# GpSimd's scale placed behind its low half, and norm weights as scalar operands, in a kernel for linear attention and a mixture of experts

## Chip, cores and metric

One core of one Trainium2 chip. The metric is the device time of one execution in microseconds (us). TensorE is PE in the profile, VectorE DVE, ScalarE ACT, GpSimd POOL, SyncE SP.

## The reference

Two parts in a row. Attention without softmax, for batch 8, 8 heads, 576 positions, head size 64:

```python
kv = np.einsum('bhsd,bhse->bhde', k, v)
out = np.einsum('bhsd,bhde->bhse', q, kv)
rms = np.sqrt(np.mean(out * out, axis=-1, keepdims=True) + 1e-06)
attn = out / rms * g_norm            # g_norm: 64 weights
```

The heads are put beside each other, which gives 4608 rows `x` of 512. Then a mixture of 8 experts: each row goes to the expert with the largest `x @ w_gate`, an expert takes at most 1152 rows, and a row's output is

```python
gate_w * (np.maximum(x @ w1[e], 0) @ w2[e])      # w1: 512 x 1024, w2: 1024 x 512
```

## The kernel before, in words

**First stage (to about 160 us).** For each batch PE makes `kv`, then the attention rows and the expert logits; VectorE and GpSimd work out the norm and the routing; each finished row goes to a scratch tensor `x_dram` in HBM as 8 heads of 64 un-normed values, each with its norm factor beside it. Rows of the expert that is picked first are worked on early.

**Second stage.** The experts are ranked by their number of rows and given fixed budgets of 704, 672, 640, 624, 592, 576, 560 and 512 rows (line 19). Experts are counted by `r` from 0. While the products of expert `r` run, two things are prepared for expert `r + 1`:

- `rows_beside` (line 1591), for tiles of 128 rows. Five steps for each tile: GpSimd gathers it with an indirect DMA into `xg` (`fetch`, line 437, four buffers); GpSimd scales it by the norm factors into `xm` (`norm`, line 444, a two-tensor product, two buffers; for `r` = 1 VectorE may do it) and copies the gate column (`gate`, line 453); ScalarE casts `xm` to float16, the high half of `pair` (`pair_high`, line 471, two buffers); GpSimd subtracts that from `xm`, the low half (`pair_low`, line 476); SyncE issues a transposing DMA from `pair` into `xs` (`pair_turn`, line 481).
- `weights` (line 1540), for `w1` and `w2`: eight pieces of 128x512 float32 each. VectorE takes the maximum of each piece (`top`, line 344, `am`); `most` (line 350) reduces the eight to one per partition, `a`, and for `w1` multiplies it by `gcol`, the column of norm weights; PE turns `a` into a row (`across`, line 357), VectorE reduces that to one number `bm` (line 361), PE spreads it to all partitions (`back`, line 364), and VectorE makes a power of two from it (`scale`, line 366), for `w1` multiplied by `gcol` again (`sg`, line 373). Then ScalarE casts each scaled piece to float16 (`high`, line 378, `w1h`, `w2h`) and VectorE makes the rest (`low`, line 384, `w1l`, `w2l`).

The products (line 1626): for each of eight blocks `j` of the hidden size PE sums three terms into a bank `hp` (line 532; two banks), ScalarE takes the relu in float16 (`hh`, line 537), and VectorE the rest (`hl`, line 540, which reads `hp` from PSUM and `hh` from SBUF). Then PE makes the tiles of the second product `yp` (lines 578 and 587), ScalarE scales them (line 603), GpSimd scatters the rows to the output (line 608).

**What sets the order.** No engine's order is chosen at run time. Each stage lists its operations with an engine, a planned duration, dependencies, a key and buffers held in rings; `Plan.place` (line 112) goes through them in planned time and always starts what can start first on an engine, by the smaller key and then by the earlier entry where several can. What it finds is the fixed order of all five instruction streams, the DMA issues on SP and POOL among them. An added dependency so changes the planned time of what follows, and with it the order of any engine from there on. The hardware still waits on semaphores where data demand it. The planned durations of the two steps on GpSimd are 1.22 us (`NORM`) and 1.33 us (`PAIR`).

Of the kernel before, what the change touches and what calls it, by code (L numbers as in the profile page):

```python
# [15 lines left out]
ALU = mybir.AluOpType  # L16
# [65 lines left out]
class Ring:  # L82
# [3 lines left out]
    def new(self):  # L86
        self.holds.append(Hold(self.holds[-self.n] if len(self.holds) >= self.n else None))
        return self.holds[-1]
# [8 lines left out]
class Plan:  # L97
# [5 lines left out]
    def op(self, ways, fn, deps=(), key=0.0, takes=(), uses=(), late=0.0):  # L103

        ways = [ways] if isinstance(ways[0], str) else list(ways)
        o = Op(ways, fn, [d for d in deps if d is not None], list(takes), key, late)
        for h in takes + uses if isinstance(takes, tuple) and isinstance(uses, tuple) else list(takes) + list(uses):
            h.users.append(o)
        self.ops.append(o)
        return o  # L110
# [56 lines left out]
def attention_moe_kernel(  # L167
# [12 lines left out]
    nc = tc.nc  # L180
# [79 lines left out]
    gcol = cst.tile([P, 1], F32, name="gcol")  # L260
# [25 lines left out]
    first = cst.tile([P, E], F32, name="first")  # L286
# [12 lines left out]
    def exponent(src, least, name, pool=sm):  # L299

        e = pool.tile([P, 1], I32, name=name)
        nc.vector.tensor_scalar(out=e, in0=src.bitcast(I32), scalar1=23, scalar2=None, op0=ALU.logical_shift_right)
        nc.vector.tensor_scalar(out=e, in0=e, scalar1=least, scalar2=None, op0=ALU.max)
        return e

    def pow2(e, mul, add, name, pool=sm):

        t = sm.tile([P, 1], I32, name="p2t")
        nc.vector.tensor_scalar(out=t, in0=e, scalar1=mul, scalar2=add, op0=ALU.mult, op1=ALU.add)
        r = pool.tile([P, 1], I32, name=name)  # L310
        nc.vector.tensor_scalar(out=r, in0=t, scalar1=23, scalar2=None, op0=ALU.logical_shift_left)
        return r.bitcast(F32)
# [18 lines left out]
    def split_weight(i, ws, raw, pieces=8):  # L331

        z = {}
        m = KD * F // pieces
        wh, wl = ws[2 * i], ws[2 * i + 1]
        sl = lambda p: slice(p * m, (p + 1) * m)

        def am():
            if "am" not in z:
                z["am"] = sm.tile([P, pieces], F32, name=f"am{i}")  # L340
            return z["am"]

        def top(p):
            nc.vector.tensor_reduce(out=am()[:, p:p + 1], in_=raw[:, sl(p)], axis=AX.X, op=ALU.max,  # L344
                                    apply_absolute_value=True)

        def sum(p):
            nc.scalar.activation(wl[:, sl(p)], raw[:, sl(p)], AF.Abs, accum_out=am()[:, p:p + 1])

        def most():  # L350
            z["a"] = a1 = sm.tile([P, 1], F32, name=f"a1_{i}")
            nc.vector.tensor_reduce(out=a1, in_=am(), axis=AX.X, op=ALU.max)
            if i == 0:
                nc.vector.tensor_tensor(out=a1, in0=a1, in1=gcol, op=ALU.mult)

        def across(pt):
            nc.tensor.transpose(pt[0:1, 0:P], z["a"], ident)  # L357

        def across_max(pt):
            z["m"] = sm.tile([1, 1], BF16, name="bm")  # L360
            nc.vector.tensor_reduce(out=z["m"], in_=pt[0:1, 0:P], axis=AX.X, op=ALU.max, apply_absolute_value=True)

        def back(pb):
            nc.tensor.matmul(pb[:, 0:1], lhsT=ones_bf, rhs=z["m"], start=True, stop=True)  # L364

        def scale(pb):
            z["b"] = sm.tile([P, 1], F32, name="bmax")
            nc.vector.tensor_copy(z["b"], pb[:, 0:1])
            z["e"] = exponent(z["b"], 30, f"ew{i}")
            z["s"] = pow2(z["e"], -1, (256, 268)[i], f"sw{i}")  # L370
            if i == 0:
                sg = sm.tile([P, 1], F32, name="sg")
                nc.vector.tensor_tensor(out=sg, in0=z["s"], in1=gcol, op=ALU.mult)  # L373
                z["s"] = sg

        def high(p, e="A"):
            if e == "A":
                nc.scalar.activation(wh[:, sl(p)], raw[:, sl(p)], AF.Copy, scale=z["s"])  # L378
            else:
                nc.gpsimd.tensor_scalar(out=wh[:, sl(p)], in0=raw[:, sl(p)], scalar1=z["s"], scalar2=None, op0=ALU.mult)  # L380

        def low(p, e="V"):
            if e == "V":
                nc.vector.scalar_tensor_tensor(out=wl[:, sl(p)], in0=raw[:, sl(p)], scalar=z["s"], in1=wh[:, sl(p)],  # L384
                                               op0=ALU.mult, op1=ALU.subtract)
            else:
                nc.gpsimd.tensor_scalar(out=raw[:, sl(p)], in0=raw[:, sl(p)], scalar1=z["s"], scalar2=None, op0=ALU.mult)
                nc.gpsimd.tensor_tensor(out=wl[:, sl(p)], in0=raw[:, sl(p)], in1=wh[:, sl(p)], op=ALU.subtract)

        return dict(top=top, sum=sum, most=most, across=across, across_max=across_max, back=back, scale=scale, high=high, low=low), z  # L390

    def split_steps(i, ws, raw, psum_pool, tag, pieces=8):
# [24 lines left out]
    def spans(s0, s1):  # L417

        cuts = [s0] + list(range((s0 // P + 1) * P, s1, P)) + [s1]
        return [(a, b - a, NHI if a % P else a // P) for a, b in zip(cuts, cuts[1:])]  # L420
# [215 lines left out]
    def slots(pool, reg_ap, s0=0):  # L636

        c_reg = nc.vector.value_load(reg_ap, min_val=0, max_val=(E - 1) * NHI)
        both = []
        for tab_, nm in ((gidx_tab, "gi"), (sidx_tab, "si")):  # L640
            t = pool.tile([P, NHI + 1], I32, name=f"{nm}{s0}", bufs=3)
            nc.vector.tensor_copy(t[:, 0:NHI], tab_[:, ds(c_reg, NHI)])  # L642
            if s0 % P:
                nc.vector.tensor_copy(t[0:P - s0 % P, NHI:NHI + 1], t[s0 % P:P, s0 // P:s0 // P + 1])
            both.append(t)
        return both
# [23 lines left out]
    op = plan.op  # L670
# [860 lines left out]
    op = plan.op  # L1531
# [59 lines left out]
    def rows_beside(r, key):  # L1591

        hold, sl, st = new("xs"), new("slots"), {}

        def cut(e):
            st["gi"], st["si"] = slots(mo, perm_i[0:1, 1, r:r + 1])

        cut_ = op(("V", 0.4), cut, [early["rank"]], key, (sl,))
        n = len(spans(0, BUDGET[r]))
        gates, turned, first, sent, asked = [], [], None, [], []  # L1600
        for i in range(n):
            xg, xm, pair = new("xg"), new("xm"), new("pair")

            def fetch(e, i=i):
                if i == 0:
                    st["x"] = Rows(mo, st["gi"], 0, BUDGET[r], BM, 4)
                st["x"].fetch(i)

            o = op(("P", 1.05), fetch, [cut_, first] + early.get(("lows", r - 1), [])[-1:], key, (hold, xg), (sl,))
            first = first or o  # L1610
            asked.append(o)
            o = op(("D", GATHER), None, [o], key, (), (xg,))
            a = op([("V", 0.61), ("P", NORM)] if r == 1 else ("P", NORM),
                   lambda e, i=i: st["x"].norm(i, nc.vector if e == "V" else nc.gpsimd), [o], key - 5 if r == 1 else key + 1,
                   (xm,), (xg,))
            gates.append(op(("P", 0.25), lambda e, i=i: st["x"].gate(i, nc.gpsimd), [a], key + 1, (), (xg, hold)))
            a = op(("A", 0.52), lambda e, i=i: st["x"].pair_high(i), [a], key + 1, (pair,), (xm, hold))
            a = op(("P", PAIR), lambda e, i=i: st["x"].pair_low(i), [a], key + 1, (), (xm, pair, hold))
            if r == 1:
                early.setdefault(("lows", r), []).append(a)  # L1620
            a = op(("S", TURN), lambda e, i=i: st["x"].pair_turn(i), [a], key + 1, (), (pair, hold))
            sent.append(a)
            turned.append(op(("D", TURNED), None, [a], key + 1, (), (pair, hold)))
        return st, hold, sl, gates, turned, sent, asked
# [50 lines left out]
    o = op(("S", 0.01), moved, [early["scaled"]], -9 * KEY, (), tuple(ews))  # L1675
# [6 lines left out]
    for r in range(E):  # L1682
        products(r, *args)
        key = KEY * r
        if r + 1 < E:
            before = [] if r > 1 else sent
            st, xs_hold, sl, gates, turned, sent, asked = rows_beside(r + 1, key + ROWS)
# [3 lines left out]
        else:  # L1691
            steps, o = plan_rest(), early["later"]
            for _ in range(68):
                o = op(("V", 0.2), lambda e: next(steps, None), [o], key + 1)
# [36 lines left out]
```

## Time and profile before

| | us |
|---|---|
| median of 3 runs | 568.02 (567.17 to 572.36) |
| profiled execution, its own time | 568.83 |
| span of its profile | 567.0 |
| PE busy | 520.8 (92%) |
| VectorE busy | 383.5 (68%) |
| ScalarE busy | 251.3 (44%) |
| GpSimd busy | 218.6 (39%) |

The span runs from the first to the last instruction. Busy time of PE is modelled and its records overlap a little, so a high share says that it is fed, not that it is at its peak. In a timeline the columns are the start, the time from there to the end of the last of the merged instructions, engine, line of the source, operation, tiles, shapes and count; in brackets stand the idle time of the engine just before and what ended it. [...]

### The profile page before, as it was taken

How to read it: one execution, taken by the hardware profiler on the slowest of the kernel's cores; microseconds unless marked ns; L12 is line 12 of the kernel's file. 1: busy time of each engine (PE TensorE's matmuls, PEld its weight loads, DVE VectorE, ACT ScalarE, POOL GpSimd, SP SyncE). 2: the span in 40 equal slices, each digit the busy share in tenths (PEclk: the TensorE clock that was granted, in tenths of full speed). 3: DMA queues.
4: the chain of work that ended last, by engine and by line, in shares of the span. 5: the costliest groups of instructions: out<-in, count | busy, mean ns of one | idle time of the engine just before them, and what ended most of it. 6: DMA issues, size and time to landing. Idle time of an engine off the chain costs nothing.

```text
span 567.0 us, 12425 instructions
## 1 busy us (share of the span) xinstructions
PE 520.8 (92%) x4727; PEld 342.4 (60%) x4727; DVE 383.5 (68%) x1009; ACT 251.3 (44%) x496; POOL 218.6 (39%) x288
## 2 busy tenths in 40 slices
PE   4999796887988997998999999999999999999994
PEld 4888685764536564544664576487467648745442
DVE  4487788999949989999998195456729606721200
ACT  1757583876313651653724435252534425202210
POOL 3012525543155583746234730644373171012011
PEclk9989996999999997999999999999999999999998
DMA  8999999654168687696947472774556151011010
GB/s 272 376 349 319 357 396 373 214 191 187 79 196 278 161 274 201 148 342 116 284 131 218 104 233 58 193 181 150 160 145 209 44 112 41 2 38 39 0 39 30
DMA packets 78020, 102.60 MB, mean 181 GB/s; under 512 B 43222, under 2 KB 51414, under 8 KB 76932
## 3 DMA queue, kind: packets, MB, share of 16 engines
q1 hardware_dynamic: 69600, 70.43, 42.8%
q0 software_dynamic: 7776, 31.30, 15.7%
q8 instruction: 39, 0.64, 0.5%
q14 instruction: 25, 0.20, 0.1%
q10 hardware_dynamic: 580, 0.02, 0.1%
HBM read 73.13 MB, written 20.61 MB: 165 GB/s over the span
## 4 chain that ended last, share of the span: by engine, by line
PE 25%; issue 15%; DMA 5%; DVE 3%; POOL 1%; ACT 1%; POOLq 0%; DVEq 0%; ACTq 0%
PE yp L578 12%; PE hp L532 12%; DMA out_dram<-ysb,si 5%; PE yp L587 1%; DVE w2l L384 1%; POOL xg L440 1%; DVE hl L540 1%; ACT w1h L378 0%; ACT w2h L378 0%; POOL xm L448 0%; POOLq L1666 0%; POOL pair L478 0%; POOL out_dram L608 0%; PE pt_max L357 0%; PE pt_max L364 0%
## 5 line engine op out<-in xcount | busy, mean ns | idle before, releaser
L532 PE MATMUL hp<-xs,w1h 128*128 128x320 f16 (+6 forms) x896 | 135.2, 303 | 4.2 <-DVE hl L540 4.2
L532 PEld LDWEIGHTS <-w1h 128*128 128x128 f16 x960 | 93.8, 99 | 48.5 <-issue 8.6
L608 POOL DMA_INDIRECT out_dram<-ysb,si x41 | 42.7, 1042 | 135.7 <-ACT ysb L603 100.0
L578 PEld LDWEIGHTS <-hh 128*128 128x128 f16 x560 | 54.4, 98 | 65.5 <-issue 3.1
L537 ACT ACTIVATE hh<-hp 128x320 f16<-128x320 f32 (+7 forms) x64 | 40.8, 638 | 113.2 <-PE hp L532 113.1
L344 DVE TENSOR_REDUCE am<-raw 128x1 f32<-128x512 f32 x120 | 75.7, 674 | 3.4 <-DMA raw<-in_moe_w_dram 3.4
L532 PE MATMUL hp<-xs,w1l 128*128 128x320 f16 (+6 forms) x448 | 72.1, 301 | 0.0
L478 POOL TENSOR_TENSOR pair<-xm,pair 128x512 f16<-128x512 f32 (+5 forms) x35 | 44.1, 1262 | 67.6 <-ACT pair L474 62.9
L540 DVE SCALAR_TENSOR_TENSOR hl<-hp,hh 128x320 f16<-128x320 f32 (+7 forms) x64 | 47.2, 737 | 32.8 <-ACT hh L537 32.6
L578 PE MATMUL yp<-w2h,hh 128*128 128x512 f16 x272 | 64.4, 379 | 0.8 <-ACT ysb L603 0.8
L578 PE MATMUL yp<-w2l,hh 128*128 128x512 f16 x272 | 64.6, 379 | 0.0
L603 ACT ACTIVATE ysb<-yp,ysc 128x512 f32<-128x512 f32 (+5 forms) x40 | 27.4, 685 | 83.8 <-PE yp L578 80.0
L578 PE MATMUL yp<-w2h,hl 128*128 128x512 f16 x272 | 64.3, 379 | 0.0
L384 DVE SCALAR_TENSOR_TENSOR w2l<-raw,sw,w2h 128x512 f16<-128x512 f32 x64 | 52.8, 869 | 11.2 <-ACT w2h L378 11.2
L440 POOL DMA_INDIRECT xg<-x_dram,gi x41 | 42.1, 1027 | 44.2 <-DVE gi L642 25.2
L532 PEld LDWEIGHTS <-w1l 128*128 128x128 f16 x480 | 47.0, 98 | 19.5
L825 PE MATMUL op<-kv_bd,qt 128*128 128x144 f32 x256 | 41.9, 303 | 6.4 <-ACT o_sb L678 1.6
L384 DVE SCALAR_TENSOR_TENSOR w1l<-raw,sg,w1h 128x512 f16<-128x512 f32 x64 | 46.7, 783 | 0.9 <-ACT w1h L378 0.8
L578 PEld LDWEIGHTS <-hl 128*128 128x128 f16 x280 | 27.0, 98 | 31.9
L378 ACT ACTIVATE w1h<-raw,sg 128x512 f16<-128x512 f32 x61 | 39.1, 711 | 7.2 <-DVE sg L373 7.1
L378 ACT ACTIVATE w2h<-raw,sw 128x512 f16<-128x512 f32 x62 | 39.6, 710 | 5.0 <-PE yp L587 3.2
L825 PEld LDWEIGHTS op<-kv_bd,qt 128*128 128x128 f32 x256 | 35.3, 198 | 10.0 <-ACT qt L678 2.7
(257 smaller groups left out, 704.2 us busy)
## 6 DMA issues: line engine op xcount, KB each, us to landing
raw<-in_moe_w_dram SPq DMA_DIRECT2D x64, 512.0 KB, 5.0
k_sb<-in_k_dram SPq DMA_DIRECT2D x16, 576.0 KB, 7.3
v_sb<-in_v_dram SPq DMA_DIRECT2D x16, 576.0 KB, 7.2
x_dram<-o_sb POOLq DMA_DIRECT2D x8, 1152.0 KB, 7.4
q_sb<-in_q_dram SPq DMA_DIRECT2D x16, 512.0 KB, 8.1
x_dram<-o_sb POOLq DMA_DIRECT2D x8, 144.0 KB, 7.3
q_sb<-in_q_dram SPq DMA_DIRECT2D x32, 32.0 KB, 6.0
xg<-x_dram,gi POOLq DMA_INDIRECT x41, 4.8
```

The lines of the kernel that those rows point to most:

```text
L344: nc.vector.tensor_reduce(out=am()[:, p:p + 1], in_=raw[:, sl(p)], axis=AX.X, op=ALU.max, apply_absolute_value=True)
L378: nc.scalar.activation(wh[:, sl(p)], raw[:, sl(p)], AF.Copy, scale=z["s"])
L384: nc.vector.scalar_tensor_tensor(out=wl[:, sl(p)], in0=raw[:, sl(p)], scalar=z["s"], in1=wh[:, sl(p)], op0=ALU.mult, op1=ALU.subtract)
L440: nc.gpsimd.indirect_dma_start(out=self.xg[i][0:n], out_offset=None, in_=x_dram[0:self.rows, :], in_offset=bass.IndirectOffsetOnAxis(ap=se ...
L478: nc.gpsimd.tensor_tensor(out=pair[0:n, 1], in0=self.xm[i][0:n], in1=pair[0:n, 0], op=ALU.subtract)
L532: nc.tensor.matmul(self.view(hp)[:, u], lhsT=w[:, c, j * P:(j + 1) * P], rhs=x[:, c, u * hw:(u + 1) * hw], start=(t == 0 and c == 0), stop ...
L537: nc.scalar.activation(self.out(self.hh, j), self.view(hp), AF.Relu)
L540: nc.vector.scalar_tensor_tensor(out=self.out(self.hl, j), in0=self.view(hp), scalar=0.0, in1=self.out(self.hh, j), op0=ALU.max, op1=ALU.s ...
L578: nc.tensor.matmul(yp[0:n, 0:DM], lhsT=h[:, j, o:o + n], rhs=w[:, j, :], start=(m == 0), stop=(m == len(self.terms) - 1))
L603: nc.scalar.activation(self.ysb[0:n], yp[0:n, 0:DM], AF.Copy, scale=self.ysc[0:n, i:i + 1])
L608: nc.gpsimd.indirect_dma_start(out=out[:, :], out_offset=bass.IndirectOffsetOnAxis(ap=self.sidx[0:n, col:col + 1], axis=0), in_=ysb[0:n], ...
L825: nc.tensor.matmul(y, lhsT=qt.t[:, i * P:(i + 1) * P], rhs=kv2[:, half * HH + i], start=True, stop=True)
```

## The change

Two edits. In `split_weight`, the two products of a one-element column with `gcol` are written as `tensor_scalar` with `gcol` as a scalar operand, where they were `tensor_tensor` with `gcol` as a second tensor. In `rows_beside`, for `r` of 2 and above, the scale of tile `i` gets a planned dependency on the low half of tile `i - 1`. Both run on GpSimd for these experts, so it is an order and needs no semaphore of its own. For `r` = 1 nothing is added.

```diff
@@ -351,7 +351,7 @@ most
             if i == 0:
-                nc.vector.tensor_tensor(out=a1, in0=a1, in1=gcol, op=ALU.mult)
+                nc.vector.tensor_scalar(out=a1, in0=a1, scalar1=gcol, scalar2=None, op0=ALU.mult)
@@ -370,7 +370,7 @@ scale
                 sg = sm.tile([P, 1], F32, name="sg")
-                nc.vector.tensor_tensor(out=sg, in0=z["s"], in1=gcol, op=ALU.mult)
+                nc.vector.tensor_scalar(out=sg, in0=z["s"], scalar1=gcol, scalar2=None, op0=ALU.mult)
@@ -1597,7 +1597,7 @@ rows_beside
-        gates, turned, first, sent, asked = [], [], None, [], []
+        gates, turned, first, sent, asked, low = [], [], None, [], [], None
@@ -1611,13 +1611,15 @@
             a = op([("V", 0.61), ("P", NORM)] if r == 1 else ("P", NORM),
-                   lambda e, i=i: st["x"].norm(i, nc.vector if e == "V" else nc.gpsimd), [o], key - 5 if r == 1 else key + 1,
+                   lambda e, i=i: st["x"].norm(i, nc.vector if e == "V" else nc.gpsimd), [o, low], key - 5 if r == 1 else key + 1,
                    (xm,), (xg,))
             gates.append(op(("P", 0.25), lambda e, i=i: st["x"].gate(i, nc.gpsimd), [a], key + 1, (), (xg, hold)))
             a = op(("A", 0.52), lambda e, i=i: st["x"].pair_high(i), [a], key + 1, (pair,), (xm, hold))
             a = op(("P", PAIR), lambda e, i=i: st["x"].pair_low(i), [a], key + 1, (), (xm, pair, hold))
             if r == 1:
                 early.setdefault(("lows", r), []).append(a)
+            else:
+                low = a
```

## Rows read from the trace of the kernel before

**Rows 1.** The page: busy tenths of PE in 40 slices of the span.
```profile
PE   4999796887988997998999999999999999999994
```

**Rows 2.** Waits of PE, 200 to 270 us, then 270 to 562 us.
```profile
PE hp L532 <- DVE hl L540: 3.8, 1, 3.8
PE pt_max L364 <- DVE bm L361: 2.2, 2, 1.2
...
PE pt_max L357 <- DVE a L354: 0.5, 1, 0.5
...
PE hp L532 <- DVE hl L540: 0.3, 1, 0.3
```

**Rows 3.** Windows: length, busy time of PE, PEld, DVE, ACT, POOL; clock, DMA.
```profile
168.80:171.60 2.80, 0.01 (x1) 0.02 (x1) 1.42 (x6) 0.00 (x0) 0.87 (x1) 1.00 1.00 392
...
219.50:225.60 6.10, 6.05 (x24) 3.36 (x24) 6.07 (x12) 0.00 (x0) 0.00 (x0) 0.54 0.52 123
```

**Rows 4.** Timeline of PE, 215 to 269 us: where it waited.
```profile
219.54 4.64 PE L532 MATMUL hp<-xs,w1h 128*128 128x336 f16 x16 [3.82 <-DVE hl L540]
...
258.02 0.27 PE L357 MATMUL pt_max<-ident,a 128*1 128x128 f32 x1 [0.55 <-DVE a L354]
...
261.19 0.16 PE L364 MATMUL pt_max<-bm,ones_bf 1*128 1x1 bf16 x1 [1.17 <-DVE bm L361]
...
268.47 0.16 PE L364 MATMUL pt_max<-bm,ones_bf 1*128 1x1 bf16 x1 [1.06 <-DVE bm L361]
```

**Rows 5.** Timeline of VectorE, 211 to 264 us.
```profile
211.17 6.30 DVE L384 SCALAR_TENSOR_TENSOR w2l<-raw,sw,w2h 128x512 f16<-128x512 f32 x1
...
218.65 0.84 DVE L540 SCALAR_TENSOR_TENSOR hl<-hp,hh 128x672 f16<-128x672 f32 x1
...
232.75 0.64 DVE L373 TENSOR_TENSOR sg<-sw,gcol 128x1 f32<-128x1 f32 x1
...
255.24 2.73 DVE L354 TENSOR_TENSOR a<-a,gcol 128x1 f32<-128x1 f32 x1
257.89 3.04 DVE L344 TENSOR_REDUCE am<-raw 128x1 f32<-128x512 f32 x5
...
263.37 2.65 DVE L373 TENSOR_TENSOR sg<-sw,gcol 128x1 f32<-128x1 f32 x1
```

**Rows 6.** Groups of VectorE by line: shortest, median, longest ns; or busy us, mean ns.
```profile
L354 DVE TENSOR_TENSOR a<-a,gcol x8: 158/160/2730, 91.8 to 412.8; 128x1 f32<-128x1 f32 x8
L373 DVE TENSOR_TENSOR sg<-sw,gcol x8: 159/160/2655, 95.4 to 431.8; 128x1 f32<-128x1 f32 x8
L412 DVE TENSOR_SCALAR ys<-y,y x9: 212/214/215, 145.9 to 522.3; 128x1 f32<-128x1 f32 x9
L569 DVE TENSOR_SCALAR ysc<-gt,ys 128x5 f32<-128x5 f32 x1 | 1.1, 1118 | 0.0
L540 DVE SCALAR_TENSOR_TENSOR hl<-hp,hh x64: 471/760/857, 176.1 to 539.7; 128x320 f16<-128x320 f32 x8, 128x672 f16<-128x672 f32 x8, 128x640 f16<-128x640 f32 x8, 128x624 f16<-128x624 f32 x8
```

**Rows 7.** Timeline of GpSimd, 211 to 266 us.
```profile
211.38 1.07 POOL L448 TENSOR_TENSOR xm<-xg 128x512 f32<-128x512 f32 x1
...
213.55 0.18 POOL L455 COPY gt<-xg 128x1 f32<-128x1 f32 x1
...
214.83 2.09 POOL L448 TENSOR_TENSOR xm<-xg 128x512 f32<-128x512 f32 x2
...
232.23 1.15 POOL L478 TENSOR_TENSOR pair<-xm,pair 128x512 f16<-128x512 f32 x1 [0.44 <-ACT pair L474]
...
255.85 2.10 POOL L448 TENSOR_TENSOR xm<-xg 128x512 f32<-128x512 f32 x2
...
264.94 1.05 POOL L448 TENSOR_TENSOR xm<-xg 112x512 f32<-112x512 f32 x1
```

**Rows 8.** Timeline of ScalarE, 209 to 213 us: the casts of two tiles.
```profile
209.05 0.62 ACT L474 CAST pair<-xm 128x512 f16<-128x512 f32 x1 [0.38 <-POOL xm L448]
...
212.48 0.62 ACT L474 CAST pair<-xm 128x512 f16<-128x512 f32 x1 [2.18 <-POOL xm L448]
```

## The prediction, made before the change was run

> **What bounds the kernel now.** I read the slices of the page first: TensorE (PE) is at nine tenths or more in nearly every slice of the second half, so the question is where it isn't [rows 1]. Its waits by stretch give the answer: from 270 us to the end it waits 0.3 us in all; between 200 and 270 us, where the second expert's products run, it waits on VectorE: 3.8 us for `hl`, 2.2 us for `bm`, 0.5 us for `a` [rows 2]. [...] In PE's order of time the waits are 3.82, 0.55, 1.17 and 1.06 us [rows 4], and 0.3 us follows at 279 us [rows 2]. In all PE loses 3.82 + 2.8 + 0.55 + 1.17 + 1.06 + 0.3 = 9.7 us in a stage that the change touches. From 280 us on nothing can be won, and a delay there has to get through a PE that waits for nobody.
>
> Then I asked why VectorE is late. One `w2l` took 6.30 us from 211.17 us, `a<-a,gcol` on a single element per partition took 2.73 us, `sg<-sw,gcol` 2.65 us [rows 5]; their medians are 0.16 us for the last two [rows 6]. GpSimd's order of time has the answer: 211.38 to 216.92 us is one unbroken run of scale, low half, gate copy, low half and two scales (first, third and last are shown), and the `w2l` ends at 217.47, 0.55 us after it; 255.85 to 257.95 is the end of another, two scales, and `a` ends at 257.97; 264.94 to 265.99 is the end of a run, and `sg` ends at 266.02 [rows 5, 7]. So a VectorE operation that reads two tensors from SBUF waits for the end of a run of GpSimd's tensor operations. `hl`, which reads one of its two from PSUM, never exceeds 0.857 us in 64 [rows 6].
>
> [...]
>
> **Part one, the order on GpSimd (experts 3 to 8).** Nothing is added or removed: the same scales of 1.06 us and low halves of 1.15 us [rows 7]. Now scale i+1 comes behind low half i. What that does to a run: low half i+1 needs its high half from ScalarE, a cast of 0.62 us [rows 8], which needs scale i+1. So after "low half, scale, gate copy" GpSimd must pause at least for that cast, and a run is 1.15 + 1.06 + 0.2 = 2.4 us instead of 5.5. It gets no gate copy, gather or write less; those can only stand in the pause.
>
> At 211 us: the cast of tile 0 ended at 209.67 [rows 8], so low half 0 can start at 211.38, where scale 1 stood, and scale 1 with its gate copy ends near 213.8. `w2l` then ends 0.55 us behind it, at 214.35. From there VectorE needed 218.65 + 0.84 - 217.47 = 2.0 us to the end of `hl` (a second `w2l` and a maximum stand between) [rows 5], so `hl` ends at 216.35 instead of 219.49. PE wanted it at 219.54 - 3.82 = 215.72 [rows 4], so 0.7 us of the 3.82 stay. A gap of 0.7 us leaves the clock alone (2.8 us did [rows 3]), so the 2.8 us of low clock goes too. PE wins 3.1 + 2.8 = 5.9 us, VectorE's own queue 3.1. Bounds: nothing, if the planner's new order lays another run across the same `w2l`; 6.6 us, if the run falls behind it; below nothing, see the last rival.
>
> What is late next: the rows themselves are not. A tile of the third expert now costs a round trip to ScalarE, about 1.15 + 1.06 + 0.2 + 0.62 and some 0.3 us of hops against 2.4 us, so five tiles come some 5 us later; their products start behind the `bm` wait at 268.47 us [rows 4], while the last low half of that expert is done at 233.4 us [rows 7]. Later experts have their rows as far ahead. The SyncE queue (transposes and weight loads) is passed in the same order; it waits with the low halves.
>
> **Part two, `gcol` as a scalar.** 16 operations of 0.16 us become `tensor_scalar` with a pointer; the nearest row, `ys`, 128x1 with two such pointers, takes 0.214 us [rows 6], so 16 x 0.05 = 0.9 us more VectorE time over the whole kernel, most of it under a saturated PE. What it can save is the wait: 2.73 - 0.2 = 2.5 us at 255.24, 2.65 - 0.2 = 2.45 at 263.37, and 0.64 - 0.2 = 0.4 in an `sg` at 232.75 [rows 5]. Bounds: the new form is not delayed at all (`ys` never exceeds 0.215), or it is delayed as before: `ysc`, also with a pointer scalar but five elements wide, took 1.118 us once, beside a GpSimd scale [rows 6]. I take the full saving: `ys` has the same one element and one tensor input.
>
> [...]
>
> **The sum.** The stage from 226 to 270 us has VectorE without a gap worth naming, so PE's gain there is bounded by VectorE's. At `a`: VectorE comes 3.1 + 0.4 + 2.5 = 6.0 us earlier, `a` ends at 257.97 - 6.0 = 251.97; PE gets there at 258.02 - 0.55 - 5.9 = 251.57 and waits 0.4 us. Five maxima stand between `a` and `bm`, as before [rows 5], so the 1.17 us wait behind it stays. PE is 6.0 us ahead. At the next `bm`, VectorE is 6.0 + 2.45 = 8.45 us ahead, PE 6.0: its 1.06 us goes, and the 0.3 us too. Gain 6.0 + 1.06 + 0.3 = 7.4 us; still lost: 0.7 + 0.4 + 1.17 = 2.3 of the 9.7. The profiled execution took 568.83 us (span 567.0 and 1.8 around it), so it would take 561.4; the median of the runs is 568.02, 0.8 below it, and on that footing the forecast is 560.6 us.
>
> **Rivals.**
> Only the scalar part works: the new order leaves some run of GpSimd over the `w2l` of 211 us (or over the six at 244 us). Then PE keeps 3.82 + 2.8 and wins 0.55 + 1.17 + 1.06 = 2.8: 565.2 us. For it: the planner decides all five engines' order anew from the first moved scale on. Against: no run can be longer than 2.4 us without a pause.
> Only the order works: the pointer form waits too. VectorE gains 3.1 us at 211 us and nothing at 255 and 263 us, and PE's 5.9 is cut to that 3.1: 564.9 us. For it the `ysc` row, against it `ys` and the width.
> No gain at all: the planner moves another two-tensor operation into the way and both savings are waited away in the dense stretch of VectorE: 568 us.
> Slower: ScalarE's order is fixed too, and a cast waits at its head for the scale, with `hh` behind it; one such wait was 2.18 us at 212.48 us [rows 8]. With the scale now behind a low half, each cast can wait 1.15 us more, and with the lost overlap some 2 us. PE has two `hp` banks, so a late `hh` stops it. The two experts whose rows fall into this stage have ten tiles; if half of the casts stop PE by 2 us, that is 10 us, and 568.0 - 2.8 + 10 = 575 us. It decides from four such stops on, where it eats the 7.4 us. Against it: ScalarE sat idle for those 2.18 us and the `hh` behind the cast stopped nobody.
>
> **How the numbers follow.** Forecast 0.52 (own range 558.3, everything of the 9.7 us won, to 562.5, where only 5.5 of it are); scalar part only 0.20; order only 0.12; no gain 0.08; slower 0.08. A measurement of this kernel tells about 1%, 5.7 us, from no change, so "faster" begins at 562.3 us: 0.53, of which nearly all is the forecast; within 1%: 0.39 (the next three, and the forecast's weak end); slower: 0.08. The range takes in the forecast and the two halves, 557.8 to 567.6 us, and leaves out the slow case and most of the case without gain.
>
> **What would show it.** Right: `sg` and `a` with a maximum near 0.2 us; no `w2l` above some 3.5 us; GpSimd's timeline in pairs "low half, scale"; PE's wait for `hl` under 1.5 us and a granted clock of 1.00 from 200 us on; a wait for `bm` of about 1 us left; all of the gain made before 280 us. Wrong: a pointer form above 1 us beside a GpSimd run; a `w2l` of 5 us or more somewhere from 200 to 290 us; PE waiting for `hp` through `hh` with ScalarE at a cast; or a gain or loss behind 280 us, where I hold PE to be saturated.

## The result, and the profile after

The changed kernel took 571.8 us (median of 22 executions, 567.28 to 576.9) against 567.99 us for the kernel before (22 executions, 563.21 to 572.36): ratio 1.0062, 95% interval 1.0036 to 1.0089. That is 3.8 us slower where I forecast 7.4 us faster. Timed again on two chips it came out at 1.0068 and at 0.9973; the experiments say why both can be true, and what stays open. The ratios here and below leave out executions more than 1.5% above the fastest of their kernel, and so differ from the quotient of the medians, which are over all executions, by up to 0.5% (on chip B, 571.43 to 568.41 is 1.0053 where the ratio is 1.0003).

Its profiled execution took 570.96 us (span 569.2). The waits of PE after, first from 200 to 270 us, then from 270 to 562 us (what PE did, what it waited for, us in total, times, longest):

```profile
PE yp L578 <- ACT ysb L603: 0.8, 1, 0.8
PE yp L598 <- DVE yt L593: 0.7, 1, 0.7
PE hp L532 <- DMA xs<-pair: 0.5, 1, 0.5
PE hp L532 <- DVE hl L540: 0.5, 1, 0.5
...
PE yp L598 <- DVE yt L593: 3.4, 1, 3.4
PE hp L532 <- DVE p2t L309: 1.6, 3, 0.8
PE hp L532 <- DVE hl L540: 1.2, 3, 0.5
PE yp L587 <- issue: 0.2, 1, 0.2
```

In the first stretch 7.2 us of waiting became 2.5 (0.7 us of it at `yt` in both; the rest of before is in [rows 2]): `hl` went from 3.8 to 0.5, `bm` and `a` are gone. In the second, 0.3 us became 6.4, over half of it one wait for `yt`. The window that was at clock 0.54 [rows 3] is at 1.00 (length, busy time of PE, clock with 1.00 for full speed, busy share of the DMA engines, GB/s):

```profile
219.22:225.60 6.38, 6.23 (x43) 1.00 1.03 258
```

VectorE's timeline of after answers to [rows 5]:

```profile
214.18 3.63 DVE L384 SCALAR_TENSOR_TENSOR w2l<-raw,sw,w2h 128x512 f16<-128x512 f32 x2
...
253.53 0.21 DVE L354 TENSOR_SCALAR a<-a,gcol 128x1 f32<-128x1 f32 x1
...
259.12 0.21 DVE L373 TENSOR_SCALAR sg<-sw,gcol 128x1 f32<-128x1 f32 x1
...
267.95 1.42 DVE L384 SCALAR_TENSOR_TENSOR w1l<-raw,sg,w1h 128x512 f16<-128x512 f32 x2 [3.94 <-ACT w1h L378]
...
270.14 0.29 DVE L593 COPY yt<-yp 128x128 f32<-128x128 f32 x1
```

Two `w2l` together take 3.63 us, where one alone took 6.30; `a` and `sg` take 0.21 us, not 2.73 and 2.65. So both parts of the change do what they say. But at 267.95 us VectorE now stands 3.94 us for ScalarE's `w1h`, and `yt`, for which PE waits, is behind that in its queue. ScalarE's casts, against [rows 8], and GpSimd's timeline, against [rows 7], say why:

```profile
244.94 0.61 ACT L474 CAST pair<-xm 128x512 f16<-128x512 f32 x1
...
254.38 0.62 ACT L474 CAST pair<-xm 128x512 f16<-128x512 f32 x1 [8.25 <-POOL xm L448]
...
260.47 0.62 ACT L474 CAST pair<-xm 128x512 f16<-128x512 f32 x1 [4.31 <-POOL xm L448]
261.00 1.95 ACT L378 ACTIVATE w1h<-raw,sg 128x512 f16<-128x512 f32 x3
266.11 0.62 ACT L474 CAST pair<-xm 128x512 f16<-128x512 f32 x1 [3.16 <-POOL xm L448]
266.63 0.68 ACT L603 ACTIVATE ysb<-yp,ysc 128x512 f32<-128x512 f32 x1
267.21 3.16 ACT L378 ACTIVATE w1h<-raw,sg 128x512 f16<-128x512 f32 x5
```

```profile
245.63 1.24 POOL L478 TENSOR_TENSOR pair<-xm,pair 128x512 f16<-128x512 f32 x1 [0.21 <-issue]
252.24 1.01 POOL L608 DMA_INDIRECT out_dram<-ysb,si  x1 [5.37 <-DMA out_dram<-ysb,si]
253.28 1.06 POOL L448 TENSOR_TENSOR xm<-xg 128x512 f32<-128x512 f32 x1
...
258.33 1.02 POOL L608 DMA_INDIRECT out_dram<-ysb,si  x1 [2.10 <-DMA out_dram<-ysb,si]
259.38 1.06 POOL L448 TENSOR_TENSOR xm<-xg 128x512 f32<-128x512 f32 x1
```

In the kernel before, the same place of GpSimd's queue was:

```profile
243.81 1.02 POOL L608 DMA_INDIRECT out_dram<-ysb,si  x1 [1.24 <-ACT ysb L603]
244.84 1.09 POOL L448 TENSOR_TENSOR xm<-xg 128x512 f32<-128x512 f32 x1
...
252.50 1.06 POOL L608 DMA_INDIRECT out_dram<-ysb,si  x1 [5.97 <-DMA raw<-in_moe_w_dram]
253.57 2.31 POOL L478 TENSOR_TENSOR pair<-xm,pair 128x512 f16<-128x512 f32 x2
```

GpSimd issues the second expert's output rows between the fourth expert's rows, and stands 5.37 us at a write until the one before it has landed. It stood so before too: the trace has the write of 243.81 us landing at 251.69, and the next begins at 252.50, though the row names another DMA as what ended the idle time. But then a scale had been done ahead of that stand (two `xm` buffers allow it); now the scale comes behind the low half, and the write has slipped in between. The cast waits 8.25 us at the head of ScalarE's queue, with two `ysb` behind it; the next two casts wait 4.31 and 3.16 us, and `w1h` stands behind these. In four waits, with a last one of 0.35, the casts lose 16 us; before, in the same stretch, none of them waited for a scale.

For the comparisons below I cut PE's time at the first `hp` product of an expert, read from PE's timelines (us; lengths of the stretches, the last one to PE's end):

```
                       1st to 2nd  2nd to 3rd  3rd to 4th  4th to end
before, first profile       28.12       66.74       53.89      237.27
after, first profile        28.69       59.51       57.63      240.93
```

7.2 us are won up to the third expert, 3.7 given back up to the fourth, 3.7 after it. The second expert also starts 2.4 us later after, 1.8 of it ahead of the first expert's products; over all twenty profiles these start between 172.1 and 177.2 us, so I put this down to the execution.

### The profile page after: what moved, and what is told of

The parts are those of the page before. It is cut to its first block, busy times and chain, and to the rows that moved or that the text cites. A ratio compares the mean times of both kernels' runs of the same rounds, so it can differ in the third digit from the quotient of the medians.

```text
span 569.2 us, 12403 instructions
## 1 busy us (share of the span) xinstructions
PE 520.2 (91%) x4727; PEld 341.5 (60%) x4727; DVE 377.4 (66%) x1009; ACT 250.6 (44%) x496; POOL 221.0 (39%) x288
## 4 chain that ended last, share of the span: by engine, by line
issue 28%; DVE 24%; PE 18%; POOL 13%; DMA 13%; ACT 2%; POOLq 0%; DVEq 0%; SPq 0%; ACTq 0%
DMA out_dram<-ysb,si 9%; DVE w2l L384 5%; PE hp L532 4%; PE yp L578 4%; POOL xg L440 3%; PE op L825 3%; POOL pair L478 3%; POOL xm L448 3%; DVE hl L540 2%; DVE ss L858 2%; PE qp L807 2%; DVE am L344 2%; POOL out_dram L608 1%; DVE w1l L384 1%; DMA v_sb<-in_v_dram 1%
## 5 line engine op out<-in xcount | busy, mean ns | idle before, releaser
L532 PE MATMUL hp<-xs,w1h 128*128 128x320 f16 (+6 forms) x896 | 133.7, 300 | 3.9 <-DVE hl L540 1.7
L478 POOL TENSOR_TENSOR pair<-xm,pair 128x512 f16<-128x512 f32 (+5 forms) x35 | 46.1, 1317 | 72.2 <-ACT pair L474 71.4
L578 PE MATMUL yp<-w2h,hl 128*128 128x512 f16 x272 | 65.6, 384 | 0.0
L440 POOL DMA_INDIRECT xg<-x_dram,gi x41 | 43.5, 1061 | 44.4 <-DVE gi L642 26.2
L384 DVE SCALAR_TENSOR_TENSOR w2l<-raw,sw,w2h 128x512 f16<-128x512 f32 x64 | 51.3, 846 | 11.8 <-ACT w2h L378 11.0
L384 DVE SCALAR_TENSOR_TENSOR w1l<-raw,sg,w1h 128x512 f16<-128x512 f32 x64 | 49.4, 824 | 6.4 <-ACT w1h L378 6.4
L474 ACT CAST pair<-xm 128x512 f16<-128x512 f32 (+5 forms) x35 | 21.4, 613 | 54.1 <-POOL xm L448 51.4
```

Source lines behind the costliest of these rows:

```text
L440: nc.gpsimd.indirect_dma_start(out=self.xg[i][0:n], out_offset=None, in_=x_dram[0:self.rows, :], in_offset=bass.IndirectOffsetOnAxis(ap=se ...
L478: nc.gpsimd.tensor_tensor(out=pair[0:n, 1], in0=self.xm[i][0:n], in1=pair[0:n, 0], op=ALU.subtract)
L532: nc.tensor.matmul(self.view(hp)[:, u], lhsT=w[:, c, j * P:(j + 1) * P], rhs=x[:, c, u * hw:(u + 1) * hw], start=(t == 0 and c == 0), stop ...
L578: nc.tensor.matmul(yp[0:n, 0:DM], lhsT=h[:, j, o:o + n], rhs=w[:, j, :], start=(m == 0), stop=(m == len(self.terms) - 1))
```

## The experiments

Five chips, A to E; ratios are to the kernel before on the same chip. Each kernel ran 12 times, the one with writes apart and the new order 6 times; there is one profile to a run.

```
kernel                        chip   us       ratio    95% interval
scalars alone                  A   567.36   0.9962   0.9927 to 0.9997
order alone                    A   572.83   1.0072   1.0027 to 1.0118
both, third expert only        A   570.6    1.0048   1.0013 to 1.0084
both, all other queues kept    A   569.83   1.0042   1.0003 to 1.008
changed kernel                 B   572.64   1.0068   1.0038 to 1.0098
scale ahead of write           B   571.43   1.0003   0.9968 to 1.0039
scalars alone                  B   568.67   0.999    0.9956 to 1.0025
writes apart, new order        C   563.79   0.9887   0.9852 to 0.9921
writes apart, old order        C   569.3    0.9972   0.9943 to 1.0
planner told, new order        C   569.25   1.0022   0.9985 to 1.0058
planner told, old order        C   571.63   1.0074   1.0037 to 1.0111
scale ahead of write           D   567.47   0.9945   0.9919 to 0.9971
changed kernel                 E   568.39   0.9973   0.9946 to 1.0
scale ahead of write           E   566.83   0.996    0.9929 to 0.999
scalars alone                  E   568.0    0.9978   0.9945 to 1.0011
```

**The parts apart (chip A).** The scalars with the old order:

```diff
-    ... [o, low], key - 5 if r == 1 else key + 1,
+    ... [o], key - 5 if r == 1 else key + 1,
```

> Only the scalar operands; every engine keeps the order of the kernel before. Theory A (the order edit costs what it wins, because casts on ScalarE now wait at its head for a scale that stands behind a GpSimd that waits): the scalar form works by itself, a and sg stay at about 0.21 us, PE loses its waits of 0.55, 1.17 and 1.06 us and keeps the 3.8 us one: 2.8 us faster, ratio 0.995. Theory B (the order costs nothing, the longer scalar operations cost time in the first 200 us, where the profile after is 2.4 us later): ratio 1.004 or more, and PE reaches the second expert's products later than 201.8 us. Theory C (the new plan of the other engines costs, not GpSimd's order): as A here.

The order with the two-tensor products kept:

```diff
...
-    nc.vector.tensor_scalar(out=sg, in0=z["s"], scalar1=gcol, scalar2=None, op0=ALU.mult)
+    nc.vector.tensor_tensor(out=sg, in0=z["s"], in1=gcol, op=ALU.mult)
```

> Only the order, with the two-tensor products by gcol kept; the plan is that of the changed kernel. A: as slow as the changed kernel or slower by up to the 2.8 us that the scalars save, ratio 1.006 to 1.011; waits of PE behind yt, p2t and hl as in the changed kernel. B: ratio about 1.000 to 1.002, since the scalar form that costs is gone. C: as A.

Both parts, the order for the third expert's rows only:

```diff
-            else:
+            elif r == 2:
                 low = a
```

> Scalars, and the order for the third expert's rows alone; the rows of the fourth to eighth are scaled ahead as before. A: the 6 us won at 211 us and the scalars' 2.8 stay, and the waits that the changed kernel has from 265 us on (3.4 us behind yt, 2.5 us behind p2t and hl later) go: ratio 0.985 to 0.990. B: ratio 1.00. C: cannot be told from A here, since the plan of the other engines changes less too.

The planner sees the old dependences; GpSimd's scales are moved behind the low halves when its plan is written out, so PE, VectorE, ScalarE and SyncE keep the order of the kernel with the scalars alone:

```diff
-        for o in self.place():
+        for o in behind(self.place(), set(self.ops)):
...
+            a.behind = low
```

> Scalars, and the order of GpSimd as in the changed kernel for the third to eighth experts, but put in after the planning: TensorE, VectorE, ScalarE and SyncE keep the order of the kernel before, instruction for instruction. A: GpSimd's order by itself makes the casts wait, so this is no better than the changed kernel, ratio 1.000 to 1.015, with the casts waiting for a scale for 15 us or more in all. C: the new plan was the cost, so this wins what I forecast: ratio 0.987. B: ratio 1.00 with a later start of the second expert's products.

The scalars alone win 0.4%; each form of the order loses 0.4 to 0.7%. Where only GpSimd's queue differs (1.0042), these are ScalarE's waits from 240 to 275 us and PE's from 200 to 285:

```profile
ACT pair L474 <- POOL xm L448: 14.6, 3, 7.6
PE pt_max L364 <- DVE bm L361: 4.5, 1, 4.5
```

This kernel has the plan of the scalars alone, so GpSimd's order by itself is enough for a loss. That doesn't clear a new plan: with the order for the third expert only, 0.985 to 0.990 was expected and 1.0048 came out. There the fourth expert's scales are done ahead as before, and yet:

```profile
ACT pair L474 <- DMA xs<-pair: 8.1, 2, 6.1
PE hp L532 <- DVE p2t L309: 5.1, 1, 5.1
```

One cast waits 6.07 us for a transposing DMA to free its `pair` buffer; `w1h` is behind the cast, VectorE stands 5.27 us for `w1h`, and PE 5.1 us for the products, the first 16 of which then take 4.14 us, where 16 of the next block take 2.34. A queue that stands at writes can so reach PE through a buffer too, in a plan that puts `w1h` behind such a cast. And the profile of the scalars alone held a surprise: the old order without the `hl` wait that was expected to stay (0.2 us in all after 200 us). PE had lost 4.1 us at `yt` just before, and so came late to the place where it would have waited.

**The two kernels profiled once more (chip C).** No edit.

> The kernel before, unchanged, profiled once more. Question: is the 3.8 us wait of PE for hl at 215 to 219 us, with the low clock behind it, a property of the kernel or of the one execution that I read? Theory 'of the kernel': PE waits 3 to 4 us for hl near 215 us again, the granted clock falls below 0.7 for some 6 us behind it, and the second expert takes about 66.7 us from its first product to the third expert's. Rival 'of that execution': PE loses some 4 us earlier, at yp behind yt near 205 us, as in the profiles of all four kernels run so far; then PE is late when it wants hl, waits under 1 us for it at a clock of 1.00, and the stretch from the second to the third expert's first product takes 60 to 63 us.

> The changed kernel, unchanged, profiled once more. Theory 'the order makes the casts late': as in the first profile of it, the casts of the fourth expert's rows (240 to 272 us) wait at the head of ScalarE's queue for GpSimd's scales, over 10 us in sum, and PE waits 2 to 4 us near 270 us for yt. Rival 'that wait was of one execution': the yt wait near 270 us is under 1 us here. Both: sg and a near 0.21 us, w2l at most 3.7 us.

Here `hl` cost 3.7 us before, at clock 0.83 over 220 to 230 us, and 0.4 after; in the changed kernel casts waited 8.35, 4.31 and 3.15 us and `yt` cost 3.4, as in its first profile. So the `hl` wait of before and the late casts of after were not of one execution. The stretches were 65.07, 55.05 and 238.15 us before, 59.54, 58.64 and 238.65 after: 5.5 us won, where the first pair of profiles, with a lower clock before, had 7.2.

**Writes that wait for none (chip C).** Each output tile of the second expert goes to a buffer of its own, so that its rows are missing from the output; in the new order, and in the old one with the scalars:

```diff
+    aside = [dram.tile([N, DM], F32, name=f"aside{i}") for i in range(NHI)]
...
-                out=out[:, :], out_offset=...
+                out=getattr(self, "to", [out] * NHI)[i][:, :], out_offset=...
...
+            if r == 1:
+                st["g2"].to = aside
```

> The changed kernel, with the second expert's output tiles each written to a buffer of its own and not to the output (so that its rows are missing from the output): the writes are issued as before, but none waits for the one before it. Theory A (the new order costs because GpSimd stands at a write that waits for the previous write, 5.4 and 2.1 us, and the scale that used to be done ahead of that now stands behind it): without those waits the casts of the fourth expert's rows wait under 5 us in sum, the yt wait near 270 us is gone, and the time is 1.5 to 3.5 us under the changed kernel's, so at most 0.3% above its twin with the old order. Theory B (the order costs by itself, each cast waits for a low half more, here and in all later experts): this kernel stays 0.7 to 1.0% above its twin. Theory C (the cost is paid behind 290 us, in the later experts, where the writes still wait): same 0.7 to 1.0%, but with the stretch from the second to the fourth expert's first product within 1 us of the twin's.

> The twin: order of before, gcol as a scalar, and the second expert's output tiles each written to a buffer of its own (its rows are missing from the output). Theory A: the old order did a scale ahead while GpSimd waited, so it had little to win here: within 0.3% of the kernel with the scalars alone (ratio to before 0.993 to 0.999). Theory B and C: the same, and 0.7 to 1.0% below the kernel with the new order and the same writes. Were the writes' waits a cost of their own in both orders, this kernel would come 0.5% or more under the scalars alone (ratio below 0.991).

This pair decides. Without the waiting writes the new order is 5.5 us faster than the old one (563.79 against 569.3). That it is near the 5.9 us I gave it is partly chance, since the stretches below are 8.1 us won and 2.4 given back, and the 8.1 have PE's 2.6 us for `a` in them, which my 5.9 left out. The waits of ScalarE in the new order, 240 to 275 us:

```profile
ACT pair L475 <- POOL xm L449: 4.7, 3, 3.3
```

and those of PE in the old order, 200 to 285 us:

```profile
PE hp L533 <- DVE hl L541: 3.7, 1, 3.7
PE pt_max L358 <- DVE a L355: 2.6, 1, 2.6
```

16.1 us of casts waiting for scales became 4.7 (3.7 more for a transposing DMA), and PE's `yt` waits 1.2 in two. The old order wins nothing from free writes that the ratios show (0.9972, against 0.9962 to 0.999 for the scalars on other chips). The stretches in the new order are 58.25, 54.75 and 238.79 us, in the old 66.31, 53.38 and 237.75: 8.1 us won, 1.4 and 1.0 given back. Theory A holds, B and C fall for the bulk; the last 1 us is as C has it.

**The planner told of the wait (chip C).** A write may start 4.5 us after the one before; the output is whole.

```diff
...
-            ... st["g2"].write(i, yh.t), [o], key, (), (yh, sl_hold))
+            ... st["g2"].write(i, yh.t), [o] + early.get("wrote", []), key, (), (yh, sl_hold))
+            early["wrote"] = [op(("W", 4.5), None, [o], key)]
```

> The changed kernel whose planner is told that a write of output rows can start only 4.5 us after the one before it was issued; it may then place a scale and a low half where GpSimd would stand at a write. All of the output is computed. Theory A (the order's gain of some 5 us is eaten by casts that wait for a scale behind a standing write): the casts of the fourth expert's rows wait under 6 us in sum, where the changed kernel had 16 us; the yt wait near 270 us is under 1 us; 1.5 to 5 us under the changed kernel, ratio to before 0.990 to 0.998. Rival 'the writes are the limit wherever they stand': the waits move to other places, the last write of the second expert lands as late, and the ratio stays 1.000 to 1.008.

> Its twin with the old order: gcol as a scalar, and the planner told of the 4.5 us between writes. Theory A: little to win, for the old order had a scale done ahead at those places: ratio to before 0.992 to 1.000, and at least 0.3% above the twin with the new order. Rival: the planner's knowledge of the writes is worth as much in either order, and this one comes out level with its twin or below it.

The new order is the better of the pair, by 2.4 us, but both are slower than hoped: 1.0022 and 1.0074. GpSimd's queue now changes from the writes ahead of the first expert's products on, and new waits appear in both (2.3 and 2.4 us at `yp` for `bmax`). Both forecasts missed, 0.990 to 0.998 and 0.992 to 1.000. In the new order the casts wait 4.7 us for scales, as hoped, but 4.7 for a transposing DMA: what the told planner wins at the writes it loses elsewhere, as far as these waits show.

**Two instructions moved (chip D).** In the changed kernel the second expert's second and third write go behind the scales of the fourth expert's third and fourth tile; all other queues stay (`behind` as above):

```diff
+            if r == 1:
+                early.setdefault("writes", []).append(o)
...
+            if r == 3 and i in (2, 3):
+                early["writes"][i - 1].behind = a
```

> The changed kernel with two instructions moved, both on GpSimd: the second and third write of the second expert's output rows are issued behind the scales of the third and fourth tile of the fourth expert's rows, and no longer ahead of the scales of the second and third tile. All other engines keep the changed kernel's order; the output is whole. Theory A (the whole loss is a scale behind a standing write): the casts of those rows wait under 6 us in sum instead of 16, the yt wait near 270 us is under 1 us, PE's stretch from the third to the fourth expert's first product is 2 to 4 us shorter, and the time is 1.5 to 4 us under the changed kernel's: ratio to before 0.990 to 0.999. Rival 'the writes are the limit wherever they stand': a write that is issued later lands later, ScalarE then waits for a free output buffer instead, and the ratio stays 1.003 to 1.009. Rival 'what was won in the kernel with writes of their own came from the DMA queues being freer': the casts no longer wait, and the time still stays within 1 us of the changed kernel's.

0.9945, inside theory A's range. GpSimd's timeline there, and then ScalarE's waits from 240 to 275 us:

```profile
244.22 1.48 POOL L448 TENSOR_TENSOR xm<-xg 128x512 f32<-128x512 f32 x1
...
247.57 1.06 POOL L448 TENSOR_TENSOR xm<-xg 128x512 f32<-128x512 f32 x1
249.31 1.05 POOL L608 DMA_INDIRECT out_dram<-ysb,si  x1 [0.69 <-DMA out_dram<-ysb,si]
257.37 0.99 POOL L608 DMA_INDIRECT out_dram<-ysb,si  x1 [6.81 <-DMA out_dram<-ysb,si]
```

```profile
ACT pair L474 <- POOL xm L448: 6.3, 3, 2.9
```

The second write stands 0.69 us instead of 5.37; the stand of 6.81 us comes one write later, with a scale already done. The casts wait 6.3 us, slightly over the 6 expected, the single `yt` wait of 3.4 us is gone (1.0 in two), and the stretch to the fourth expert is 56.38 us, 1.3 and 2.3 under the changed kernel's two profiles above, where 2 to 4 were expected. The changed kernel wasn't timed on this chip.

**All three on one chip (chip B).** The changed kernel, this last version and the scalars alone, unchanged, and the kernel before with a profile.

> The changed kernel, unchanged, timed again, now beside its two rivals on one chip. Theory A (its order costs what it wins, and more): ratio to before 1.002 to 1.009, as in the first timing; casts of the fourth expert's rows wait over 10 us in sum, PE's yt wait near 270 us is 3 us or more. Rival 'it depends on the chip': on chips where PE doesn't lose 4 us at yt near 205 us the changed kernel wins 0.3% or more.

> The changed kernel with the two writes behind the scales, unchanged from its first run, on the same chip as the changed kernel. Theory A: 0.5 to 1.5% under the changed kernel, ratio to before 0.990 to 0.998. Rival 'the first ratio came from its chip': within 0.3% of the changed kernel.

> The kernel with the scalars alone, unchanged from its first run, on the same chip as the other two. Theory A: ratio to before 0.993 to 1.000, at least 0.4% under the changed kernel. Rival 'its first ratio came from its chip, where yt stood 4 us': level with before (0.999 to 1.002).

> The kernel before, profiled on the chip of the three others. If the 4 us at yt near 205 us belong to a chip, all four profiles of this chip agree on it. If they belong to an execution, they differ. Where they are there, I expect PE's wait for hl near 215 us to be under 1 us; where not, 3.7 to 3.8 us.

The order of the three is as expected, but the moved writes missed their 0.990 to 0.998. By the ratios they are worth 0.65% over the changed kernel, with intervals that touch; by the medians 0.2%, which leaves them 0.5% behind the kernel before. The scalars' 0.999 fits both theory A and its rival. The profile of the kernel before on this chip shows why so little is won (PE's waits, 200 to 285 us; then VectorE's timeline):

```profile
PE yp L598 <- DVE yt L593: 4.2, 1, 4.2
PE pt_max L364 <- DVE bm L361: 2.2, 2, 1.2
PE hp L532 <- DVE hl L540: 0.3, 1, 0.3
```

```profile
204.56 0.42 DVE L593 COPY yt<-yp 128x256 f32<-128x256 f32 x1 [3.41 <-remote]
...
216.06 1.52 DVE L384 SCALAR_TENSOR_TENSOR w2l<-raw,sw,w2h 128x512 f16<-128x512 f32 x2
```

VectorE idles 3.41 us ahead of a `yt` copy, PE 4.2; after that the queues stand so that the two `w2l` take 1.52 us, not 6.96 as in the first profile, and `hl` costs 0.3 us. There is little here for the order to win: the second to third stretch is 60.78 us before and 59.03 after, the next 53.88 and 59.48. Of these 5.6 us about 3 are PE's `yt` wait, and most of the rest is the low clock behind it (0.66 in the changed kernel from 270 to 280 us, 1.00 before). In the version with the moved writes GpSimd is idle for 6.97 us ahead of one write here, and PE waits 4.0 us at `yp` for `sw`; that they were moved by hand to fit the waits of another chip may be why, which no run tests. All eight profiles of chips A and B have this wait (3.3 to 3.4 us of VectorE), none of the seven of chips C and D, nor the first two, whose chip isn't known.

**A fifth chip (E).** The same three kernels.

> The changed kernel once more, with the same two companions as on the last chip. What I hold now: a chip shows one of two pictures at 200 to 220 us. Where yt waits 3.4 us near 205 us (two chips so far, nine profiles), the kernel before has no hl collision to lose, the order wins nothing and only costs: ratio 1.003 to 1.010. Where yt doesn't wait (two chips, seven profiles), the order wins about 7 us up to the third expert and gives back 4 to 6: ratio 0.993 to 1.002. Rival: the picture at 205 us doesn't matter for the whole, and the ratio is 1.003 to 1.009 in either.

> The changed kernel with the two writes behind the scales. Where yt waits near 205 us: 0.997 to 1.004, as on the last chip. Where it doesn't: 0.991 to 0.998, as in its first run. In both at least 0.2% under the changed kernel.

> The scalars alone. Where yt waits near 205 us: 0.993 to 1.002. Where it doesn't, PE waits 3.7 us for hl as in the kernel before, and the ratio is 0.993 to 1.000. Were the scalars worth the 2.8 us that I gave them, 0.995.

(The first of these texts counts nine and seven profiles; they are eight and seven. Its two pictures, with and without the `yt` wait, are meant below too.) Chip E shows no `yt` wait, and the changed kernel comes out at 0.9973, as the split by picture says. VectorE with the old order and the scalars, and then with the new:

```profile
213.46 6.94 DVE L384 SCALAR_TENSOR_TENSOR w2l<-raw,sw,w2h 128x512 f16<-128x512 f32 x2
```

```profile
216.26 3.63 DVE L384 SCALAR_TENSOR_TENSOR w2l<-raw,sw,w2h 128x512 f16<-128x512 f32 x2
```

The stretches are 65.43, 53.77 and 237.19 us with the scalars alone, 60.09, 57.13 and 240.08 with the changed kernel: 5.3 won, 3.4 and 2.9 given back. The scalars alone are at 0.9978 and the moved writes at 0.996, both in their ranges; the moved writes were to be at least 0.2% under the changed kernel and are 0.13% under it. Between these three the intervals don't separate.

## Why the prediction was wrong

- **The run of GpSimd on `w2l` at 211 us: right, with its price, on chips without the `yt` wait.** `hl` went from 3.82 to 0.46 us (I left 0.7), the clock from 0.54 to 1.00, the stretch from the second to the third expert from 66.74 to 59.51 us, 7.2 where the sum, with the scalars, has 7.1 up to there. The 2.8 us for the clock in the sum are an estimate from [rows 3], 6.1 x (1 - 0.54); in the same trace the 24 products of that window take 6.32 us from 219.54, the next 24, at 1.00, 3.58 us from 225.69: 2.7 us. On chip C, where the clock fell less (0.83 over 10 us), it was 5.5. "A gap of 0.7 us leaves the clock alone" came true at 219 us, behind a wait of 0.46 us, and is no rule: in the kernel before on chip C, PE waited 1.16 and 1.06 us near 264 and 271 us, and the clock was at 0.83 from 270 to 280.
- **The same term on chips with it: next to nothing instead of 5.9.** I read it off one execution. On chips A and B PE loses 4 us just ahead of the place, and there the kernel before waits 0.3 us for `hl` (the profile on chip B). My bound "nothing" stood for a new plan that lays another run across `w2l`; the reason found is another one.
- **The pointer scalars: mechanism right, size about half.** The 16 take 0.214 us on average, also beside GpSimd: four of them overlap one of its operations, such as `a` at 253.53 us under the scale of 253.28 us. None takes over 0.215 us, the longest `ys` of [rows 6], from which I took the full saving; in the same profile one of the two `ysc` of five elements from 211.02 us, beside the scale of 210.97 us, took 1.03 us. No run changes the width alone. For the whole kernel I gave 2.8 us; three chips measured 0.1 to 0.4%, 0.6 to 2.2 us, clear of no change on chip A alone. Part of PE's waits for `bm` stays (1.8 us on chip E).
- **The failed step: "What is late next: the rows themselves are not."** I let five tiles come some 5 us later and looked at when the third expert's rows are needed. For the fourth expert I wrote that its rows are as far ahead, and didn't follow what else stands in GpSimd's queue there: the writes, one with an idle time of 5.97 us ahead of it, another of 2.21. I counted GpSimd's instructions as work and not as places where it stands. The rows were indeed not needed earlier; but a late scale holds ScalarE's whole queue, and the path is cast, `w1h`, `w1l`, `yt`, PE. It cost 3.4 us at `yt` and 0.8 at `ysb` in the first profile, and 3.4 to 5.6 us of the stretch to the fourth expert on chips B, C and E, the 5.6 with the low clock in them; 0.5 to 2.9 us more are lost behind it. So the 7.4 us of the forecast were met by a loss that the sum had at nothing, and the median came out 11.2 us above the forecast.
- **The slower rival had the mechanism, and the wrong place.** It had the cast at the head of ScalarE's queue, waiting for a scale behind a low half, with `hh` behind it and PE stopped through `hp`. What stood behind was `w1h`, and a wait per cast is not a low half of 1.15 us but a low half and a standing write, up to 8.25 in the first profile. I argued it away with one wait of 2.18 us that stopped nobody [rows 8], taken where GpSimd stood at no write.
- **"From 280 us on nothing can be won, and a delay has to get through a PE that waits for nobody."** Not quite: 0.5 to 3.7 us are lost behind the fourth expert's start, and I had named a loss behind 280 us as a sign of being wrong. PE's waits there, all but 0.2 us at `hp` for VectorE's `hl` and `p2t`, grew from nothing to 2.5 us in the first pair and to 2.1 on chip E, which is over two thirds of the loss there, but by 0.7 on chip B and 0.2 on chip C, half or less of it.

What is left open: why the `yt` copy waits on chips A and B (the trace names no instruction that releases it), and why the first timing, whose profile shows the picture without it, has the ratio of the chips with it; which chip each of those 22 executions ran on isn't known. That the picture decides whether the whole is faster or slower rests on chip E against chips A and B. Why `hl` and `p2t` come late behind the fourth expert's start isn't traced.

The best whole version is the changed kernel with the two writes moved: faster than before on two chips (0.9945, 0.996), on a third level by the ratio (1.0003) and 0.5% slower by the medians. The scalars alone cost nothing anywhere. With writes that wait for none the changed kernel, scalars included, was 1.1% faster than the kernel before on chip C.

## What to carry to other kernels

Before an instruction is moved behind another on an in-order engine, list every place in between where that engine stands still, DMA waits of issuing instructions above all, and ask which of the work it used to do ahead of the stand now falls behind it. A buffer that lets one stage run ahead is worth something at every stand that it covers: here the second `xm` had covered one of over 5 us. And a wait read off one execution should be seen on a second chip before it is put into a sum: in the old order the largest term was there in the first profile and on chips C and E, and not on A and B.

## What the hardware showed that was not expected

- One kernel has two pictures, by chip as far as it was profiled: 3.3 to 3.4 us of VectorE idle ahead of one `yt` copy near 205 us in all eight profiles of two chips, none in those of three others. Median times of the kernel before hardly differ (568.3 and 568.41 against 569.22 to 570.86 us), as they would if the one wait stood in for the other.
- Taking away a wait of a DMA on the DMA before it is worth nothing with one order of the queue (0.9972, with the writes waiting 0.9978 on chip E) and about 0.9% with the other (0.9887, with the writes waiting 0.9973 on chip E).
- A VectorE operation held by GpSimd was held to the end of its unbroken run, here as in [rows 5, 7]: in the old order with free writes, six `w2l` in a row took 10.16 us from 247.13 us, where eight take 7.42 in the new order with the same writes; GpSimd's run of two low halves and two scales went from 252.37 to 256.73 us, and the last `w2l` ended at 257.29.
